# A SwiGLU block on one core: a split load of x, other PSUM banks for two small groups, and two sums of h moved

## The chip, the core and the metric

The kernel runs on one core of a Trainium2 chip. The core's engines work side by side and each has its own instruction queue, which it executes in order: TensorE (PE in the profile) for matrix products, VectorE (DVE), ScalarE (ACT) and GpSimd (POOL) for element-wise work, and SyncE (SP), whose queue issues most of the transfers. SBUF is the on-chip memory of 128 partitions, and PSUM the accumulators that TensorE writes, in eight banks of 128 x 512 fp32. Engines wait for each other by semaphores. The metric is the device time of one execution in microseconds.

## The reference

x has 2048 tokens of width 512, and the inner width is 1376. All inputs and the output are bf16.

```python
B, S, D, F = 1, 2048, 512, 1376
# x: (B, S, D)   w_gate, w_up: (D, F)   w_down: (F, D)
def reference(x, w_gate, w_up, w_down):
    g = silu(x @ w_gate)
    u = x @ w_up
    return (g * u) @ w_down
```

## The kernel before

x is brought in transposed (`xT_sb`), so that the contraction lies on partitions, in four chunks of 512 tokens: c = 0 to 3. F is cut into ten blocks of 128 (`ft` 0 to 9) and a tail of 96. Gate and up products of a block go into PSUM banks. ScalarE makes silu of the gate, and VectorE or GpSimd multiplies by up and writes h in bf16: `h0_sb` for tokens 0-1023, `h1_sb` for tokens 1024-2047.

Most products are made by Winograd's form of Strassen's scheme, with seven block products in place of eight for a 2 x 2 block problem. It needs sums of the weights (S1 to S4 and a cast A22) and sums of the tokens (T1 to T4 and a cast B22), kept as fp32r. In the gate/up phase a `Unit` (L581) treats two neighbouring blocks for two chunks of tokens. There are eight units: three for the first half of the tokens (u = 2, 4, 3) and five for the second (u = 0, 2, 4, 3, 1). The blocks 0 to 3 of the first half are made directly, by `classic` (L455). A unit's products run in the order p6, p5, p7, p2, then p1 of the next unit, then p3, p4. Banks X alternate between (0, 1) and (2, 3), Y is (4, 5), W is (6, 7). VectorE empties them: two `ts` sums for W after p5 and p7, an h product for Y, a copy of one X bank to Y, two more `ts` sums for W after p3, and an h product for X. GpSimd multiplies the `ts` sums into h.

The sums of weights are made by GpSimd into `ss_sb`, four slots that the units use in turn (`w_sums`, L531). The sums of tokens 0-1023 are made by VectorE into `tt_sb[0]`, those of tokens 1024-2047 by GpSimd into `tt_sb[1]` (`x_sums`, L555).

The down phase (`down`, L938) makes tokens 1024-2047 directly, tile by tile (`body`, L701), and tokens 0-1023 again by Strassen, in two `DownUnit`s (L833) whose operands are sums of w_down (S1 to S4, `s_sum`, L782) and sums of `h0_sb` (T1 to T4, `t_sum`, L796). Those sums lie in places that are free by then. S1 and S2 are made by GpSimd in the slot of u = 2, S3 and S4 by VectorE in the slot of u = 4. T1 and T2 are made by VectorE in `tt_sb[1]`, which the last unit still reads; T3 and T4 in `th_sb`, which shares its place with the weights `w_sb`. B22 lies in the slot of u = 3. Each T sum is three instructions: one block pair (128 x 512) and twice two (128 x 1024). `p1`'s result is read by VectorE (`keep`, the `r_sb` rows) before `p6` may add into the same bank.

The order of work on TensorE and SyncE is written out by hand (L992-L1038). For the other engines a planner (`Plan.schedule`, L58) works out an order from costs in ns, dependences and priorities: it always takes the operation that can start first. The T sums have the lowest priority, 9, so they go where an engine is idle in the plan. `land` is when the planner takes a load to have arrived; it changes the order only, the waits themselves are on semaphores.

Loads (L264-L319) are issued on SyncE in the order: xn (tokens 0-255), gate and up weights of the first blocks with tokens 256-511 between them, weights of blocks 2 and 3, tokens 512-1023 in one transposing load (`x1`, L293), and the rest. After the work on chunk 0, TensorE makes blocks 0, 1 and 2 of chunk 1 (L998), then the groups of the F tail, each in a bank b (L1013-L1020): `plan_x(c, b)` for its 96 gate columns and last 32 up columns of one chunk, and `plan_y(pi, b)` for its first 64 up columns of two chunks. Then come the units.

## Time and profile before

| | us |
|---|---|
| median of 3 runs | 116.96 (116.81 to 117.84) |
| the profiled execution, its own time | 116.91 |
| its span in the trace | 115.6 |
| TensorE busy | 111.7 |
| VectorE busy | 78.7 |
| ScalarE busy | 63.8 |
| GpSimd busy | 58.5 |

The profile is that of one execution. Each engine's busy time is the time in which it executes instructions other than waits. In the rows of the timeline the first number is the start from the beginning of the span, the second the length, both in us; then engine, line, operation, the tile written and those read, partitions x elements, and how many neighbouring instructions of one kind are merged in the row (x20). The bracket at the end gives the idle time before the row and what ended it. "PEld" is the loading of weights into TensorE, which overlaps its products. A row of the stretches has begin and end, length, then for PE, PEld, DVE, ACT and POOL the busy time and the number of instructions, then TensorE's granted clock (1.00 throughout here), the DMA share and GB/s.

### The profile page before, as it was taken

The numbers are of one execution on the slowest core, as the hardware profiler recorded it, in microseconds if no ns is written. First come the engines' busy times: TensorE is split into PE (matmuls) and PEld (weight loads), VectorE is DVE, ScalarE is ACT, GpSimd is POOL, SyncE is SP. The second block draws the span as 40 slices with busy tenths as digits, with TensorE's granted clock in tenths as the row PEclk, the third lists the DMA queues.
The fourth block names the chain that finished last, engine by engine and source line by source line (L and its number), as shares of the span: only waits on it lengthen the run. The fifth ranks groups of instructions, "written<-read, shape, count | busy, mean of one in ns | idle before, by whom it ended". The sixth has DMA issues, their size and how long they took to land.

```text
span 115.6 us, 1763 instructions
## 1 busy us (share of the span) xinstructions
PE 111.7 (97%) x650; PEld 69.0 (60%) x650; DVE 78.7 (68%) x115; ACT 63.8 (55%) x123; POOL 58.5 (51%) x55
## 2 busy tenths in 40 slices
PE   7999999999999999999999999999999799999993
PEld 2565566546675858576776858643435356866452
DVE  0122999773956859393949577599999997476423
ACT  5344765896778776767677787820767940000000
POOL 1069004999999999958999979144000000000000
PEclk9999999999999999999999999999999999999999
DMA  3999999993000000000000000000121002228896
GB/s 84 267 239 233 324 196 223 305 339 82 0 0 0 3 0 3 0 0 6 0 0 3 0 0 0 0 0 0 62 80 45 0 0 45 45 51 136 177 267 191
DMA packets 22776, 9.84 MB, mean 85 GB/s; under 512 B 12816, under 2 KB 22640, under 8 KB 22768
## 3 DMA queue, kind: packets, MB, share of 16 engines
q1 hardware_dynamic: 20624, 8.69, 31.2%
q10 hardware_dynamic: 2144, 1.05, 3.9%
q8 instruction: 5, 0.08, 0.3%
q14 instruction: 3, 0.02, 0.1%
HBM read 4.75 MB, written 2.10 MB: 59 GB/s over the span
## 4 chain that ended last, share of the span: by engine, by line
PE 72%; DVE 15%; DMA 7%; SPq 3%; issue 1%
PE psum L595 31%; PE psum L607 12%; PE psum L843 9%; DMA xT_sb<-in_x_dram 7%; PE psum L705 6%; DVE tt_sb L336 6%; PE psum L410 5%; DVE th_sb L336 4%; PE psum L474 3%; PE psum L855 3%; SPq L267 2%; PE psum L421 1%; PE psum L500 1%; DVE ss_sb L336 1%; SPq L279 1%
## 5 line engine op out<-in xcount | busy, mean ns | idle before, releaser
L595 PE MATMUL psum<-tt_sb,ss_sb 128*128 128x512 f32 x160 | 40.3, 404 | 0.0
L595 PEld LDWEIGHTS psum<-tt_sb,ss_sb 128*128 128x128 f32 x160 | 29.9, 188 | 7.8 <-DVE psum L325 0.4
L336 DVE TENSOR_TENSOR ts_sb<-r_sb,psum 128x512 f32<-128x512 f32 x32 | 20.5, 681 | 15.0 <-ACT r_sb L324 15.0
L336 POOL TENSOR_TENSOR h_sb<-sg_sb,ts_sb 128x512 bf16<-128x512 f32 x16 | 20.6, 1286 | 6.7 <-ACT sg_sb L331 6.7
L324 ACT ACTIVATE r_sb<-psum 128x512 f32<-128x512 f32 x32 | 17.3, 594 | 5.5 <-PE psum L595 5.5
L331 ACT ACTIVATE sg_sb<-psum 128x512 f32<-128x512 f32 x24 | 14.3, 598 | 10.7 <-PE psum L595 7.1
L336 DVE TENSOR_TENSOR h_sb<-sg_sb,psum 128x512 bf16<-128x512 f32 x24 | 16.4, 682 | 5.5 <-PE psum L410 5.5
L705 PE MATMUL psum<-wd_sb,h_sb 128*128 128x512 bf16 (+2 forms) x100 | 18.4, 337 | 0.0
L336 POOL TENSOR_TENSOR ss_sb<-w_sb 128x512 fp32r<-128x512 bf16 x10 | 11.4, 1157 | 13.5 <-DVE tt_sb L336 7.3
L607 PE MATMUL psum<-xT_sb,w_sb 128*128 128x512 bf16 x64 | 15.4, 381 | 0.0
L705 PEld LDWEIGHTS psum<-wd_sb,h_sb 128*128 128x128 bf16 x100 | 8.3, 98 | 9.2 <-issue 1.0
L410 PE MATMUL psum<-xT_sb,w_sb 128*64 128x512 bf16 (+1 forms) x128 | 12.8, 353 | 0.5 <-DMA xT_sb<-in_x_dram 0.3
L331 ACT ACTIVATE sg_sb<-ts_sb 128x512 f32<-128x512 f32 x16 | 10.1, 633 | 2.1 <-DVE ts_sb L336 2.1
L410 PEld LDWEIGHTS psum<-xT_sb,w_sb 128*64 128x64 bf16 x128 | 7.5, 110 | 5.4 <-issue 0.7
L607 PEld LDWEIGHTS psum<-xT_sb,w_sb 128*128 128x128 bf16 x64 | 5.5, 98 | 8.0 <-issue 2.5
L843 PE MATMUL psum<-tt_sb,ss_sb 128*128 128x512 f32 x20 | 5.6, 417 | 0.6 <-DVE r_sb L336 0.6
L325 DVE COPY psum<-psum 128x512 f32<-128x512 f32 x8 | 5.6, 699 | 0.7
L336 POOL TENSOR_TENSOR ss_sb<-w_sb,ss_sb 128x512 fp32r<-128x512 bf16 x5 | 5.8, 1169 | 0.2
L325 DVE CAST o_sb<-psum 128x512 bf16<-128x512 f32 (+2 forms) x6 | 3.0, 513 | 4.2 <-PE psum L705 3.1
L336 POOL TENSOR_TENSOR ss_sb<-ss_sb,w_sb 128x512 fp32r<-128x512 f32 x5 | 5.8, 1161 | 0.0
L843 PE MATMUL psum<-th_sb,ss_sb 128*128 128x512 f32 x20 | 5.5, 413 | 0.0
L855 PE MATMUL psum<-h_sb,wd_sb 128*128 128x512 bf16 x20 | 5.0, 381 | 0.0
(71 smaller groups left out, 121.7 us busy)
## 6 DMA issues: line engine op xcount, KB each, us to landing
wd_sb<-in_w_down_dram SPq DMA_DIRECT2D x1, 1280.0 KB, 9.0
w_sb<-in_w_gate_dram SPq DMA_DIRECT2D x4, 256.0 KB, 4.4
w_sb<-in_w_up_dram SPq DMA_DIRECT2D x4, 256.0 KB, 4.7
out_dram<-o_sb SPq DMA_DIRECT2D x7, 128.0 KB, 1.8
out_dram<-xT_sb ACTq DMA_DIRECT2D x4, 128.0 KB, 3.2
out_dram<-xT_sb ACTq DMA_DIRECT2D x2, 256.0 KB, 3.1
w_sb<-in_w_gate_dram SPq DMA_DIRECT2D x1, 352.0 KB, 5.2
w_sb<-in_w_up_dram SPq DMA_DIRECT2D x1, 320.0 KB, 5.7
```

Of the source, the lines that this page charges most:

```text
L267: lambda e: e.dma_start(w_sb[:, :, m, c0:c0 + f1 - f0], src[:, f0:f1].rearrange("(k p) f -> p k f", p=P)),
L324: return e.activation(out, src, ACT.Copy)
L325: return e.tensor_copy(out, src)
L331: "A", lambda e: e.activation(out, src, ACT.Silu), reads, writes, busy, A_LAG, prio
L336: engs, lambda e: e.tensor_tensor(out, a, b, alu), reads, writes, busy,
L410: ins = e.matmul(psum[h:h + HC, b, n0:n1], lhsT=w_sb[:, dk, m, ft * P + h:ft * P + h + HC], rhs=xT_sb[:, dk, c * SC + n0:c * SC + n1], sta ...
L474: ins = e.matmul(psum[m:m + HC, b, :], lhsT=w_sb[:, dk, 0, XC0 + m:XC0 + m + HC], rhs=xT_sb[:, dk, c * SC:(c + 1) * SC], start=(dk == 0), ...
L595: ins = e.matmul(bank(dst), lhsT=s[:, k, :], rhs=t[:, k, :], start=(start and k == 0), stop=(k == KH - 1), skip_group_check=True,)
L607: ins = e.matmul(bank(dst), lhsT=w_sb[:, k0 + k, m, f:f + P], rhs=xT_sb[:, k0 + k, c:c + SC], start=(start and k == 0), stop=(k == KH - 1) ...
L705: ins = e.matmul(psum[:, b, 0:c1 - c0], lhsT=hrows(F_ORDER[n], t, 0, P), rhs=wd_sb[:, F_ORDER[n], c0:c1], start=(start and n == n0), stop= ...
L843: ins = e.matmul(bank(dst), lhsT=self.ds[s][:, j, self.q, :], rhs=self.dt[t][:, j, :], start=(start and n == 0), stop=(n == NFF // 2 - 1), ...
L855: ins = e.matmul(bank(dst), lhsT=wd_sb[:, 2 * j + a, d * P:(d + 1) * P], rhs=h0_sb[:, 2 * j + a, 0:SC], start=(n == 0), stop=(n == NFF // ...
```

## The change

- Tokens 512-1023 are loaded by two transposing loads of 256 tokens, `x1a` and `x1b`. TensorE makes gate and up of blocks 0 and 1 for the first 256 of these tokens, four groups, and then for the other 256. Block 2 follows whole, as before.
- The tail groups use other banks: `plan_y(0)` 4 in place of 2, `plan_x(2)` 5 in place of 4, `plan_x(3)` 2 in place of 5.
- For the down blocks, T1 lies in the `ss_sb` slot of u = 4 and T3 in that of u = 3. Both are free before the last unit ends. Each is made of five instructions of 128 x 512. S3 and S4 move to the beginning of `tt_sb[1]`, B22 to `th_sb`. The order given is T1, T3, T2, S3, T4, S4.
- The planner's landing times are others, and eight semaphore numbers are no longer set aside, so that the loads take others.

```diff
-        s_out = [take(i) for i in (8, 1, 2, 3, 4, 5, 7, 6)]
...
-            plan.add(...).land = landed + (0 if landed < 5000 else 500 if landed < 10000 else 500)
+            plan.add(...).land = landed + 300
...
-                ... [name], 1500, 5.2 * (t1 - t0)
+                ... [name], 1500, (6.5 if SC <= t0 < 2 * SC else 4) * (t1 - t0)
...
-        load_x("x1", SC, 2 * SC)
+        for i in range(2):
+            load_x(f"x1{'ab'[i]}", SC + i * HT, SC + (i + 1) * HT)
...
         def x_keys(c):
+            if c == 1:
+                return ["x1a", "x1b"]
...
-            slots |= {n: (slot_of[U_ORDER[1][2]], i) for i, n in enumerate(("S3", "S4"))}
...
-            dt["T1"], dt["T2"], dt["T3"], dt["T4"] = tile(tt1, 0), tile(tt1, 1), th_sb[:, 0, :, :], th_sb[:, 1, :, :]
-            dt["B22"] = tile(flat(slot_of[U_ORDER[1][3]]), 0)
-            free = {"T1": before([("tt", 1, n, k) for n in X_SUM.values() for k in range(KH)])}
-            free["T2"] = free["T1"]
-            free["T3"] = free["T4"] = before([f"w{g}{a}" for g in "gu" for a, _ in slabs] + ["wut"])
-            free["B22"] = used(slot_of[U_ORDER[1][3]])
+            ds["S3"], ds["S4"] = wide(tt1, 0), wide(tt1, 1)
+            for n, u in (("T1", 2), ("T3", 3)):
+                dt[n] = tile(flat(slot_of[U_ORDER[1][u]]), 0)
+            dt["T2"], dt["T4"], dt["B22"] = tile(tt1, 1), th_sb[:, 0, :, :], th_sb[:, 1, :, :]
+            free = {n: used(slot_of[U_ORDER[1][u]]) for n, u in (("T1", 2), ("T3", 3))}
+            free |= {n: used(s) for n, (s, i) in slots.items()}
+            free["S3"] = free["S4"] = free["T2"] = before([("tt", 1, n, k) for n in X_SUM.values() for k in range(KH)])
+            free["T4"] = free["B22"] = before([f"w{g}{a}" for g in "gu" for a, _ in slabs] + ["wut"])
...
-                for j0, j1 in ((0, 1), (3, 5), (1, 3)):
+                for j0, j1 in ((0, 1), (3, 5), (1, 3)) if n in ("T2", "T4") else [(j, j + 1) for j in range(NJ)]:
...
             t_sum("T1")
+            t_sum("T3")
             t_sum("T2")
-            t_sum("T3")
-            s_sum("S3", "D", [t_ops["T3"]])
+            s_sum("S3", "D", [t_ops["T2"]])
...
-        for ft in early[:3]:
-            classic(1, [ft])
+        pairs = [(m, ft, next_bank()) for ft in early[:2] for m in range(2)]
+        for i in range(2):
+            for m, ft, b in pairs:
+                pe(
+                    gu_emit(m, ft, 1, b, range(KD), i * HT, (i + 1) * HT), [f"x1{'ab'[i]}", f"w{'gu'[m]}{slab_of[ft]}"],
+                    [("b", b)], 2,
+                )
+        for n, ft in enumerate(early[:2]):
+            classic_out(ft, 1, pairs[2 * n][2], pairs[2 * n + 1][2])
+        classic(1, early[2:3])
...
-        plan_y(0, 2)
-        y_out(0, 2)
-        plan_x(2, 4)
-        plan_x(3, 5)
+        plan_y(0, 4)
+        y_out(0, 4)
+        plan_x(2, 5)
+        plan_x(3, 2)
```

With this the planner gives VectorE the following order from the second last unit on (line numbers of the changed kernel; the `ss_sb<-h0_sb` rows are T1 and T3):

```
65 L336 TensorTensor ss_sb<-h0_sb 128x512 x4
66 L336 TensorTensor ts_sb0<-r_sb2,psum 128x512
67 L336 TensorTensor ts_sb1<-r_sb3,psum 128x512
68 L336 TensorTensor h1_sb<-sg_sb3,psum 128x512
69 L336 TensorTensor ts_sb2<-r_sb0,psum 128x512
70 L325 TensorCopy psum<-psum 128x512
71 L336 TensorTensor ts_sb3<-r_sb1,psum 128x512
72 L336 TensorTensor h1_sb<-sg_sb5,psum 128x512
73 L336 TensorTensor ss_sb<-h0_sb 128x512 x3
74 L336 TensorTensor ts_sb0<-r_sb0,psum 128x512
75 L336 TensorTensor ts_sb1<-r_sb1,psum 128x512
76 L336 TensorTensor h1_sb<-sg_sb1,psum 128x512
77 L336 TensorTensor ss_sb<-h0_sb 128x512
78 L336 TensorTensor ts_sb2<-r_sb4,psum 128x512
79 L336 TensorTensor ts_sb3<-r_sb5,psum 128x512
80 L336 TensorTensor h1_sb<-sg_sb2,psum 128x512
81 L336 TensorTensor ss_sb<-h0_sb 128x512 x2
82 L336 TensorTensor tt1_sb<-h0_sb,ss_sb 128x512
83 L336 TensorTensor tt1_sb<-h0_sb,ss_sb 128x1024 x2
```

GpSimd's order there is: an S1 sum, an h product, the other S1 sum, an h product, both S2 sums, then the last four h products. Before, an h product stood between the two S2 sums. In the first unit VectorE's bank copy (L325) comes ahead of an `hl`, the second `hty` and another `hl` product, where it stood behind the first two of these.

More of the change, by code (lines that the diff above doesn't have):

```diff
@@ L258, in load @@
             i = take(homes[name] if name in homes else rest[0])
-            plan.add("S", emit, writes=writes, busy=busy, lag=1800, dma=(i, 16)).land = landed + (0 if landed < 5000 else 500 if landed < 10000 else 500)
+            plan.add("S", emit, writes=writes, busy=busy, lag=1800, dma=(i, 16)).land = landed + 300
         slabs = [(0, 2), (2, 4), (4, 6), (6, 8), (8, NFF + 1)]
@@ L278, in load_x @@
             load(
-                name, lambda e: e.dma_start_transpose(xT_sb[:, :, t0:t1], xf[t0:t1, :]), [name], 1500, 5.2 * (t1 - t0)
+                name, lambda e: e.dma_start_transpose(xT_sb[:, :, t0:t1], xf[t0:t1, :]), [name], 1500, (6.5 if SC <= t0 < 2 * SC else 4) * (t1 - t0)
             )
@@ L770, in down_sums @@
             ds, dt = {}, {}
-            for n, (s, i) in slots.items():
-                ds[n] = flat(s)[:, i * HALF:(i + 1) * HALF].rearrange("p (j q c) -> p j q c", j=NJ, q=2)
+            wide = lambda a, i: a[:, i * HALF:(i + 1) * HALF].rearrange("p (j q c) -> p j q c", j=NJ, q=2)
             tt1 = tt_sb[1][:, :, :, :].rearrange("p n k c -> p (n k c)")
             tile = lambda a, i: a[:, i * NJ * SC:(i + 1) * NJ * SC].rearrange("p (j t) -> p j t", j=NJ)
-            dt["T1"], dt["T2"], dt["T3"], dt["T4"] = tile(tt1, 0), tile(tt1, 1), th_sb[:, 0, :, :], th_sb[:, 1, :, :]
-            dt["B22"] = tile(flat(slot_of[U_ORDER[1][3]]), 0)
-            free = {"T1": before([("tt", 1, n, k) for n in X_SUM.values() for k in range(KH)])}
-            free["T2"] = free["T1"]
-            free["T3"] = free["T4"] = before([f"w{g}{a}" for g in "gu" for a, _ in slabs] + ["wut"])
-            free["B22"] = used(slot_of[U_ORDER[1][3]])
+            for n, (s, i) in slots.items():
+                ds[n] = wide(flat(s), i)
+            ds["S3"], ds["S4"] = wide(tt1, 0), wide(tt1, 1)
[6 more added lines that the diff above has]
+            free["T4"] = free["B22"] = before([f"w{g}{a}" for g in "gu" for a, _ in slabs] + ["wut"])
             def s_sum(n, eng, after):
@@ L792, in s_sum @@
                         eng, at(n), a, b, alu, ["wd"] + [("ds", o, q) for o in of_], [("ds", n, q)], 9,
-                        1600 if eng == "G" else 780, used(slots[n][0]) + after,
+                        1600 if eng == "G" else 780, free[n] + after,
                     )
             def t_sum(n):
-                for j0, j1 in ((0, 1), (3, 5), (1, 3)):
+                for j0, j1 in ((0, 1), (3, 5), (1, 3)) if n in ("T2", "T4") else [(j, j + 1) for j in range(NJ)]:
                     at = lambda n: dt[n][:, j0:j1, :]
@@ L822, in casts @@
                 for q in range(2):
-                    cast_op("A", ds["A22"][:, :, q, :], wview[:, 1, 1, :, q, :], ["wd"], [("ds", "A22", q)], 9, 600, used(slots["A22"][0]) + after)
+                    cast_op("A", ds["A22"][:, :, q, :], wview[:, 1, 1, :, q, :], ["wd"], [("ds", "A22", q)], 9, 600, free["A22"] + after)
                 for j in range(NJ):
@@ L939, in down @@
             N2, N3 = NST // 2, NST // 2 + TPC
-            x_used = before([f"x{c}" for c in range(1, NSC)] + x_keys(0))
+            x_used = before([k for c in range(NSC) for k in x_keys(c)])
             for n0, n1 in ((0, NFF - 2), (NFF - 2, NFF)):
```

## The prediction

> **What bounds the kernel now.** I read the page's engine shares first, then the busy time by stretches, then the chain of waits. All times are of the profiled execution (span 115.6 us, its own time 116.91 us; the median of the runs, 116.96 us, is 0.05 us more, so sums against it carry over).

> ```profile
> PE 111.7 (97%) x650; PEld 69.0 (60%) x650; DVE 78.7 (68%) x115; ACT 63.8 (55%) x123; POOL 58.5 (51%) x55
> ```
> ```profile
> 25.40:74.60 49.20, 49.20 (x217) 34.34 (x216) 33.38 (x55) 36.64 (x72) 44.60 (x39) 1.00 0.04 8
> ...
> 76.00:91.40 15.40, 14.79 (x99) 6.30 (x97) 15.40 (x18) 8.56 (x16) 1.57 (x2) 1.00 0.11 35
> ```
> ```profile
> 4.75 7.56 DMA xT_sb<-in_x_dram
> 12.31 0.14 issue
> 12.45 5.37 PE psum L410 x48
> ...
> 90.70 0.61 DVE r_sb L336
> 91.31 0.04 issue
> 91.36 1.43 PE psum L843 x5
> ```

> TensorE (PE) is busy for 97% of the span. From 25.4 to 74.6 us it never stops (49.20 of 49.20 us), while GpSimd (POOL) is busy for 44.60 and VectorE (DVE) for 33.38. So a change gains only at the few places where PE stands, and it loses wherever it makes PE stand in the long middle. The chain shows two places: the load of x 512-1023 before 12.45, and VectorE before 91.36, at the end of a stretch where DVE works 15.40 of 15.40 us. How much each is worth comes from PE's timeline, because matmuls overlap and the idle shown is less than the time lost.

> ```profile
> 4.73 7.47 PE L410 MATMUL psum<-xT_sb,w_sb 128*64 128x256 bf16 x80
> 12.45 5.37 PE L410 MATMUL psum<-xT_sb,w_sb 128*64 128x512 bf16 x48 [0.25 <-DMA xT_sb<-in_x_dram]
> 17.62 1.92 PE L474 MATMUL psum<-xT_sb,w_sb 128*64 128x512 bf16 x16
> ...
> 25.34 3.51 PE L595 MATMUL psum<-tt_sb,ss_sb 128*128 128x512 f32 x12
> 28.69 1.90 PE L607 MATMUL psum<-xT_sb,w_sb 128*128 128x512 bf16 x8
> 30.24 5.01 PE L595 MATMUL psum<-tt_sb,ss_sb 128*128 128x512 f32 x20
> 35.09 1.90 PE L607 MATMUL psum<-xT_sb,w_sb 128*128 128x512 bf16 x8
> ...
> 68.30 4.91 PE L595 MATMUL psum<-tt_sb,ss_sb 128*128 128x512 f32 x20
> ...
> 73.74 2.21 PE L595 MATMUL psum<-tt_sb,ss_sb 128*128 128x512 f32 x8
> ...
> 89.93 0.82 PE L705 MATMUL psum<-wd_sb,h_sb 128*128 128x512 bf16 x3
> 91.36 1.43 PE L843 MATMUL psum<-tt_sb,ss_sb 128*128 128x512 f32 x5 [0.61 <-DVE r_sb L336]
> ```

> **x 512-1023 in two loads.** Without a wait a group starts 0.20 before the end shown for the one ahead (12.45 + 5.37 = 17.82, next at 17.62). The 80 matmuls end at 12.20, so the next could start at 12.00 and starts at 12.45: 0.45 us lost. Now the first half is enough to go on, and the second is needed 32 half matmuls later. The cost of halves: the 48 whole ones take 5.17 us from start to start, 0.108 each, so 32 whole ones cost 3.45 and 64 halves 3.45 at half price. From above: of the 80 in 7.27 us, 48 at 0.108 leave 2.10 for 32 halves, 0.066 each, which for 64 is 0.75 more; but that stretch holds waits of 0.3 and 0.2 us for loads (first two rows below), without which it is 0.05 each. I take 0, and 0 to 0.75 for the range.

> ```profile
> PEld psum L410 <- DMA w_sb<-in_w_up_dram: 0.3, 1, 0.3
> ...
> PEld psum L410 <- DMA xT_sb<-in_x_dram: 0.2, 1, 0.2
> ...
> PEld psum L595 <- DVE psum L325: 0.4, 1, 0.4
> ...
> PEld psum L595 <- DVE h_sb L336: 0.3, 1, 0.3
> ```
> ```profile
> 1.66 1.32 SPq L279 DMA_TRANSPOSE xT_sb<-in_x_dram  x1
> ...
> 4.75 3.91 SPq L279 DMA_TRANSPOSE xT_sb<-in_x_dram  x1
> ```

> On SyncE's queue the load holds 3.91 us as one piece; two pieces of 256 tokens hold between 2 x 1.32 and the same 3.91, so the loads queued behind it (weights, x 1024-2047) leave no later: 0. VectorE's sums of x need both halves and start when the whole would have landed: 0. Loads take other semaphores, the planner other landing times, and the two casts' tiles other homes: no instruction is added, 0. Gain 0.45.

> **Other banks.** The order of the changed kernel puts VectorE's bank copy (L325) ahead of two small products at the first unit. The 12 matmuls at 25.34 take 3.35 us to the next group, against 4.85 for 20 at 30.24, that is 2.91 for 12: 0.44 lost, by the last two waits quoted above. The first wait goes. The second, for the h product that frees bank 7, stays, as that product still stands behind the two small ones. I take 0.2 (0 to 0.44). The other tail groups get banks whose readers are one or more groups back: 0.

> **Two sums of h made early.** T1 and T3, ten VectorE instructions of 128x512, leave the stretch after 75 us. There they were these:

> ```profile
> 78.57 3.78 DVE L336 TENSOR_TENSOR tt_sb<-h_sb 128x512 fp32r<-128x512 bf16 x3
> ...
> 85.14 2.35 DVE L336 TENSOR_TENSOR th_sb<-h_sb 128x1024 fp32r<-128x1024 bf16 x2
> 87.41 0.68 DVE L336 TENSOR_TENSOR th_sb<-h_sb,tt_sb 128x512 fp32r<-128x512 bf16 x1
> ```

> Some 6.0 us leave (3.78 + 2.35, less overlaps). Two pieces of 0.6 stay, the first still blocked for about 0.8 as the first of the three is here (3.78 - 2.35 - 0.6). The second half of T4 (1.2) and the last two S4 sums (640 wide, by their width some 0.75 each) now come ahead of the r product that PE waits for. So that comes 6.0 - 2.0 - 2.7 = 1.3 us sooner, this wait goes, and what is late next is PE itself. It is worth 91.36 against 90.55 (89.93 + 0.82 - 0.20), 0.8, less the slower first step of such a group: I take 0.7 (0.6 to 0.8). Behind 91.36 the chain is PE to the end, so the gain lasts.

> The price is where the sums go. The order puts four T1 pieces behind the h product that here ends at 65.29, three more behind that of 70.91, and one where T3's first piece was already. VectorE runs in order: behind the four stand ts products that empty banks 6 and 7, and PE's group at 68.30 writes those.

> ```profile
> 64.61 0.68 DVE L336 TENSOR_TENSOR h_sb<-sg_sb,psum 128x512 bf16<-128x512 f32 x1
> 67.12 1.28 DVE L336 TENSOR_TENSOR ts_sb<-r_sb,psum 128x512 f32<-128x512 f32 x2 [1.83 <-ACT r_sb L324]
> ...
> 70.91 0.68 DVE L336 TENSOR_TENSOR h_sb<-sg_sb,psum 128x512 bf16<-128x512 f32 x1
> 73.42 1.29 DVE L336 TENSOR_TENSOR ts_sb<-r_sb,psum 128x512 f32<-128x512 f32 x2 [1.83 <-ACT r_sb L324]
> ...
> 75.22 1.63 DVE L336 TENSOR_TENSOR th_sb<-h_sb 128x512 fp32r<-128x512 bf16 x1
> ```
> ```profile
> 63.99 1.41 POOL L336 TENSOR_TENSOR ss_sb<-wd_sb 128x640 fp32r<-128x640 bf16 x1
> 65.37 1.28 POOL L336 TENSOR_TENSOR h_sb<-sg_sb,ts_sb 128x512 bf16<-128x512 f32 x1
> 66.61 1.39 POOL L336 TENSOR_TENSOR ss_sb<-ss_sb,wd_sb 128x640 fp32r<-128x640 f32 x1
> ...
> 69.97 1.42 POOL L336 TENSOR_TENSOR ss_sb<-ss_sb,wd_sb 128x640 fp32r<-128x640 f32 x1
> ```
> ```profile
> 75.03 1.28 POOL L336 TENSOR_TENSOR h_sb<-sg_sb,ts_sb 128x512 bf16<-128x512 f32 x1 [2.39 <-ACT sg_sb L331]
> ```

> The idle time is 1.83 us, and pieces alone take 0.68 and follow each other every 0.60 (two ts in 1.28). But the one sum of h that ran beside POOL took 1.63: POOL's product ended at 76.31, the sum at 76.85, so it did its 0.68 from 76.17 on, 0.14 before POOL's end, and nothing before. An instruction of VectorE that reads two SBUF tensors waits out POOL's. The ts and h products read one operand from PSUM and run undisturbed beside POOL (0.68 each).

> [...]

> At 65.29 POOL is full: it works on the S sum of 63.99, with the h product behind it, then two S sums back to back in the new order. Taking turns, on this trace's clock: T1's first piece holds from 65.26 (65.40 - 0.14), POOL's h product from 65.86 to 67.00 (0.60 later, 1.28 - 0.14), the second piece from 67.00, the S sum 67.60 to 68.85, the third piece from 68.85, the S sum 69.45 to 70.73, the fourth to 71.33. The first ts then ends at 72.01, where PE wanted its bank at 68.30: **3.7 us lost**. This takes POOL's rows to move with PE's when the early gains move those; if POOL stays, up to 0.65 more is lost here. At the second place POOL has only h products left, so one can block: 3 x 0.60 and up to 1.15 in an idle time of 1.9, ts up to 1.0 late, against some 0.75 of slack (ts ends 74.10, the last unit's four matmuls from 73.74 take about 1.1 first): 0 to 0.3, I take 0.15.

> Sum: 116.91 - 0.45 - 0.2 + 3.7 + 0.15 - 0.7 = **119.4 us**. With one POOL instruction fewer let in (1.25) it is 118.2; with no early gain, or with POOL staying, 120.1.

> **Rivals.**

> *VectorE keeps its turn.* Once it has the port, the four pieces run on end and POOL waits. For it: consecutive VectorE instructions overlap by 0.08 us, so POOL may find no gap; against it: 75.22 shows that a waiting engine gets the port at once, 0.14 before the other's end. The pieces then run from 65.26 to 67.66, ts ends at 68.34 instead of 68.30: 0.1 lost. POOL's delay costs nothing: the S sums it has still to make are first used at 91.36. 116.91 - 0.45 - 0.2 + 0.1 - 0.7 = 115.7 us, on the faster side. It decides from the second piece on: whether that starts 0.60 after the first or some 1.7.

> *Two and two.* The port changes hands only once in the group: two pieces to 66.46, POOL's h product to 67.60, two pieces to 68.80, ts to 69.48, 1.2 lost: 116.8 us.

> *The split does nothing.* If the first half lands no earlier than the whole (7.56 us of landing, all in one busy queue), PE waits at 12.00 as before and both early gains go, with VectorE keeping its turn: 116.3 us. Against it: the load is at the end of a queue that serves in order, and half of it needs only to be 0.3 us sooner.

> **How the numbers follow.** Taking turns 0.50 (119.4, own range 118.2 to 120.1), VectorE keeps its turn 0.33 (115.7, 115.3 to 116.3), two and two 0.10, no split 0.07. I put turns first because the one contended row shows a wait for a whole instruction, ended at once when the other was through. A measurement here can tell about 1% (1.17 us): below 115.8 is faster. Of the 0.33 some 0.20 lie below it, the rest with the 0.17 of the last two within 1%: faster 0.20, same 0.30, slower 0.50. The range runs from 115.5 to 120.1 and leaves out the low end of the second case and the high end of the first.

> **What would show it.** Right: T1 pieces in the VectorE rows near 65 us of 1.6 us and more each, PE idle 3 to 4 us for ts at the group now at 68.30, and no idle time before the groups now at 12.45 and 91.36. Wrong: four pieces in 2.5 us with POOL's h product stretched or moved instead; or PE's idle time where the small-product wait was, at 25 us, grown; or the 0.6 us before 91.36 still there, with T4 or a cast as its new cause.

## The result and the profile after

| | us |
|---|---|
| the changed kernel, median of 6 runs | 122.39 (121.36 to 123.49) |
| the kernel before beside it, median of 6 runs | 117.40 (116.63 to 119.45) |
| ratio, 95% interval | 1.040 (1.031 to 1.049): slower |
| the profiled execution, its own time and span | 123.49, 122.1 |

The forecast was 119.4 (115.5 to 120.1): the side and the mechanism came true, the size did not. The page of the changed kernel, its busy times and two rows of its 40 slices (each digit a busy share in tenths, and the clock granted to TensorE in tenths of full speed):

```profile
PE 114.1 (93%) x674; PEld 73.1 (60%) x682; DVE 84.0 (69%) x119; ACT 64.8 (53%) x123; POOL 59.9 (49%) x55
...
PE   7799999999999999999999907999999999999993
...
PEclk9999999999999999999999995899999999999999
```

PE's share fell from 97% to 93%: there is one hole, about 70 to 73 us, and right behind it two slices in which the clock was not full (digits 5 and 8). Before, every digit of the clock row was 9. The timeline of PE shows the same hole by its rows (start, length, ..., idle time and what ended it):

```profile
5.12 14.22 PE L412 MATMUL psum<-xT_sb,w_sb 128*64 128x256 bf16 x160 [0.68 <-DMA w_sb<-in_w_gate_dram]
...
25.33 1.89 PE L423 MATMUL psum<-xT_sb,w_sb 128*128 128x512 bf16 x8
...
31.82 4.54 PE L597 MATMUL psum<-tt_sb,ss_sb 128*128 128x512 f32 x18
...
68.33 1.90 PE L609 MATMUL psum<-xT_sb,w_sb 128*128 128x512 bf16 x8
73.93 6.38 PE L597 MATMUL psum<-tt_sb,ss_sb 128*128 128x512 f32 x20 [3.70 <-DVE ts_sb L336]
...
80.83 2.29 PE L597 MATMUL psum<-tt_sb,ss_sb 128*128 128x512 f32 x8
82.96 4.73 PE L707 MATMUL psum<-wd_sb,h_sb 128*128 128x512 bf16 x20
...
97.83 1.51 PE L847 MATMUL psum<-tt_sb,ss_sb 128*128 128x512 f32 x5
```

In this execution the first weights came late (the wait of 0.68) and the first products ran at half pace for longer (10 in the microsecond from 5 us on, 21 in the kernel before): the group at 25.33 starts at 23.49 in keep_busy3, a run of the next section with the same loads. These 1.8 us at the start are met with the loads of the kernel before too (early_t and banks_only below), and are left out by counting from anchors behind them. The anchors are groups that both traces have; the rows of before stand in the prediction, but for two, from the same view of the kernel before:

```profile
23.81 1.89 PE L421 MATMUL psum<-xT_sb,w_sb 128*128 128x512 bf16 x8
...
75.79 1.47 PE L705 MATMUL psum<-wd_sb,h_sb 128*128 128x512 bf16 x6
```

| stretch, start to start | before | after | difference |
|---|---|---|---|
| 23.81 to 30.24 (after 25.33 to 31.82), where the banks changed | 6.43 | 6.49 | +0.06 |
| to 68.30 (73.93), the group behind the first place | 38.06 | 42.11 | +4.05 |
| to 73.74 (80.83), the last unit's group | 5.44 | 6.90 | +1.46 |
| to 91.36 (97.83), the group that waited for r | 17.62 | 17.00 | -0.62 |
| to the end of the span | 24.24 | 24.27 | +0.03 |

That is +4.98. The gain of the split load lies ahead of the first anchor and is taken from the experiments (0.41, worked out below by the steps of the sum), so an undisturbed execution comes to 116.91 - 0.41 + 4.98 = 121.5 us. Three of the six runs took 121.36, 121.61 and 121.88.

The second largest line, +1.46, was in no step of the forecast. PE works all through it, only slowly, as the busy times by stretches show (begin and end, length, PE busy and matmuls, granted clock, DMA share, GB/s):

```profile
70.45:73.87 3.42, 0.00 (x0) 1.00 0.00 0
73.87:77.28 3.41, 3.35 (x8) 0.50 0.00 0
77.28:80.69 3.41, 3.34 (x16) 1.00 0.00 0
```

Behind the 3.42 us without a matmul the granted clock is 0.50 for 3.41 us: 8 matmuls where the next stretch has 16. PE's busy time cannot tell the two apart (3.35 and 3.34); the clock column and the count can.

The wait itself is made by VectorE and GpSimd. Their timelines in the changed kernel:

```profile
66.79 6.48 DVE L336 TENSOR_TENSOR ss_sb<-h_sb 128x512 fp32r<-128x512 bf16 x4
73.19 1.27 DVE L336 TENSOR_TENSOR ts_sb<-r_sb,psum 128x512 f32<-128x512 f32 x2
```
```profile
66.02 1.42 POOL L336 TENSOR_TENSOR ss_sb<-wd_sb 128x640 fp32r<-128x640 bf16 x1
67.39 1.74 POOL L336 TENSOR_TENSOR h_sb<-sg_sb,ts_sb 128x512 bf16<-128x512 f32 x1
69.08 3.64 POOL L336 TENSOR_TENSOR ss_sb<-ss_sb,wd_sb 128x640 fp32r<-128x640 f32 x2
```

Four sums that take 0.60 each alone took 6.40 from the first start to the ts product behind them, 1.6 each. GpSimd's instructions became longer too: 1.74 in place of 1.28, 1.8 in place of 1.39. Each stood for one sum of VectorE, then VectorE's next sum stood for it: turns, one for one, the four sums at 1.19, 1.77, 1.88 and 1.88. Of what the prediction calls the port, the traces show these waits and no more.

### The profile page after: what moved, and what is told of

Same layout as the page of the kernel before. It is cut to its first block, busy times and chain, and to the rows that moved or that the text cites. A ratio compares the mean times of both kernels' runs of the same rounds, so it can differ in the third digit from the quotient of the medians.

```text
span 122.1 us, 1821 instructions
## 1 busy us (share of the span) xinstructions
PE 114.1 (93%) x674; PEld 73.1 (60%) x682; DVE 84.0 (69%) x119; ACT 64.8 (53%) x123; POOL 59.9 (49%) x55
## 3 DMA queue, kind: packets, MB, share of 16 engines
HBM read 4.75 MB, written 2.10 MB: 56 GB/s over the span
## 4 chain that ended last, share of the span: by engine, by line
PE 77%; DVE 12%; issue 4%; DMA 3%; POOL 1%; ACT 1%; SPq 0%; POOLq 0%
PE psum L597 24%; PE psum L412 12%; PE psum L707 11%; PE psum L847 9%; PE psum L609 9%; DVE ss_sb L336 6%; PE psum L859 4%; DMA w_sb<-in_w_gate_dram 3%; PE psum L476 3%; DVE ts_sb L336 3%; PE psum L735 2%; DVE h_sb L336 2%; PE psum L423 1%; PE psum L502 1%; POOL h_sb L336 1%
## 5 line engine op out<-in xcount | busy, mean ns | idle before, releaser
L597 PE MATMUL psum<-tt_sb,ss_sb 128*128 128x512 f32 x160 | 41.8, 415 | 3.8 <-DVE ts_sb L336 3.7
L597 PEld LDWEIGHTS psum<-tt_sb,ss_sb 128*128 128x128 f32 x160 | 31.0, 196 | 12.4 <-DVE ts_sb L336 4.4
L336 DVE TENSOR_TENSOR ts_sb<-r_sb,psum 128x512 f32<-128x512 f32 x32 | 20.5, 680 | 11.2 <-ACT r_sb L324 11.1
L336 POOL TENSOR_TENSOR h_sb<-sg_sb,ts_sb 128x512 bf16<-128x512 f32 x16 | 21.1, 1320 | 10.9 <-ACT sg_sb L331 10.8
L336 DVE TENSOR_TENSOR h_sb<-sg_sb,psum 128x512 bf16<-128x512 f32 x24 | 16.4, 681 | 8.4 <-PE psum L412 7.6
L331 ACT ACTIVATE sg_sb<-psum 128x512 f32<-128x512 f32 x24 | 14.4, 599 | 14.2 <-PE psum L597 8.4
L324 ACT ACTIVATE r_sb<-psum 128x512 f32<-128x512 f32 x32 | 17.3, 595 | 5.5 <-PE psum L597 5.5
L336 POOL TENSOR_TENSOR ss_sb<-w_sb 128x512 fp32r<-128x512 bf16 x10 | 11.4, 1160 | 15.3 <-DVE tt_sb L336 8.9
L412 PE MATMUL psum<-xT_sb,w_sb 128*64 128x256 bf16 (+1 forms) x160 | 14.2, 348 | 0.7 <-DMA w_sb<-in_w_gate_dram 0.7
L609 PE MATMUL psum<-xT_sb,w_sb 128*128 128x512 bf16 x59 | 14.2, 380 | 0.4 <-issue 0.2
L331 ACT ACTIVATE sg_sb<-ts_sb 128x512 f32<-128x512 f32 x16 | 10.1, 633 | 5.8 <-DVE ts_sb L336 5.8
L412 PEld LDWEIGHTS psum<-xT_sb,w_sb 128*64 128x64 bf16 x160 | 10.9, 124 | 3.8 <-DVE xT_sb L325 0.9
L336 DVE TENSOR_TENSOR ss_sb<-h_sb 128x512 fp32r<-128x512 bf16 x10 | 13.0, 1348 | 0.0
L325 DVE COPY psum<-psum 128x512 f32<-128x512 f32 x8 | 5.6, 699 | 0.6
L336 POOL TENSOR_TENSOR ss_sb<-w_sb,ss_sb 128x512 fp32r<-128x512 bf16 x5 | 5.9, 1174 | 0.2
L325 DVE CAST o_sb<-psum 128x512 bf16<-128x512 f32 (+2 forms) x6 | 3.0, 512 | 4.2 <-PE psum L707 3.1
L336 POOL TENSOR_TENSOR ss_sb<-ss_sb,w_sb 128x512 fp32r<-128x512 f32 x5 | 5.8, 1168 | 0.0
L324 ACT ACTIVATE psum<-psum 128x512 f32<-128x512 f32 x8 | 4.8, 602 | 0.3 <-PE psum L609 0.2
L336 DVE TENSOR_TENSOR xT_sb<-r_sb,psum 128x512 bf16<-128x512 f32 x6 | 4.0, 687 | 1.2 <-PE psum L859 0.7
(74 smaller groups left out, 121.9 us busy)
```

The source lines that it names most:

```text
L324: return e.activation(out, src, ACT.Copy)
L325: return e.tensor_copy(out, src)
L331: "A", lambda e: e.activation(out, src, ACT.Silu), reads, writes, busy, A_LAG, prio
L336: engs, lambda e: e.tensor_tensor(out, a, b, alu), reads, writes, busy,
L412: ins = e.matmul(psum[h:h + HC, b, n0:n1], lhsT=w_sb[:, dk, m, ft * P + h:ft * P + h + HC], rhs=xT_sb[:, dk, c * SC + n0:c * SC + n1], sta ...
L597: ins = e.matmul(bank(dst), lhsT=s[:, k, :], rhs=t[:, k, :], start=(start and k == 0), stop=(k == KH - 1), skip_group_check=True,)
```

## The experiments

What each part is worth by itself came first.

**Without the sums of h (split_banks).** The changed kernel with T1 to T4, S3, S4 and B22 where and when they were before:

```diff
...
-            for n, u in (("T1", 2), ("T3", 3)):
-                dt[n] = tile(flat(slot_of[U_ORDER[1][u]]), 0)
...
+            dt["T1"], dt["T2"], dt["T3"], dt["T4"] = tile(tt1, 0), tile(tt1, 1), th_sb[:, 0, :, :], th_sb[:, 1, :, :]
...
```

> The split load, the half groups, the bank changes and the renumbered semaphores, with T1 to T4 as in the kernel before. Turns theory (the whole loss comes from the early sums): no wait before the first group on tokens 512-767, and 116.9 - 0.45 - 0.2 = 116.3 us, ratio 0.99 to 1.00. Rival (the halves cost: in the changed kernel's profile the L412 groups took 14.04 us from first to next against 12.89): 118 us, ratio 1.01, with the half groups slower than 0.054 us a matmul.

116.56 us, ratio 0.998 (0.995 to 1.002). PE's timeline in it:

```profile
4.39 12.83 PE L412 MATMUL psum<-xT_sb,w_sb 128*64 128x256 bf16 x160
...
24.75 1.75 PE L597 MATMUL psum<-tt_sb,ss_sb 128*128 128x512 f32 x6
26.65 1.66 PE L597 MATMUL psum<-tt_sb,ss_sb 128*128 128x512 f32 x6 [0.16 <-DVE h_sb L336]
28.16 1.90 PE L609 MATMUL psum<-xT_sb,w_sb 128*128 128x512 bf16 x8
...
90.82 1.43 PE L845 MATMUL psum<-tt_sb,ss_sb 128*128 128x512 f32 x5 [0.61 <-DVE r_sb L336]
```

All 160 products run without a wait for x. The 12 products of the first unit take 3.41 from 24.75 to 28.16, against 3.35 before: the first of two waits is gone and the second is longer by as much. The wait of 0.61 for r stays, so it is the sums of h that remove it. The slow-down needs those sums too. Against the kernel before beside it, 116.85, the two early parts are worth some 0.3 us, which the interval does not tell from nothing.

**The sums of h alone (early_t).** The kernel before with only that part of the change (the diff above, the other way round).

> Only the sums of h moved; loads, groups and banks as in the kernel before. Turns theory with the clock's fall: 116.9 + 3.9 (wait for ts) + 1.6 (half clock for 3.4 us behind it) + 0.15 - 0.7 = 121.9 us, ratio 1.04. Rival (a good part of the loss is the split's): below 120.7 us.

122.46 us, 1.049 (1.042 to 1.056). PE's timeline, VectorE's four sums listed by tile (count; shortest, median and longest in ns; first and last start), and GpSimd's timeline:

```profile
73.63 6.42 PE L595 MATMUL psum<-tt_sb,ss_sb 128*128 128x512 f32 x20 [3.71 <-DVE ts_sb L336]
```
```profile
L336 DVE TENSOR_TENSOR ss_sb<-h_sb x4: 677/678/4698, 66.5 to 72.3; 128x512 fp32r<-128x512 bf16 x4
```
```profile
65.25 1.41 POOL L336 TENSOR_TENSOR ss_sb<-wd_sb 128x640 fp32r<-128x640 bf16 x1
66.63 1.28 POOL L336 TENSOR_TENSOR h_sb<-sg_sb,ts_sb 128x512 bf16<-128x512 f32 x1
67.88 2.75 POOL L336 TENSOR_TENSOR ss_sb<-ss_sb,wd_sb 128x640 fp32r<-128x640 f32 x2
```

The whole loss is in this part. And here there were no turns: the first sum was out for 4.70 us, while GpSimd ran three instructions on end at their usual length; then came the other three sums at 0.68. The wait is the same within 0.01 (3.71, and 3.70 above), since either way all that GpSimd has queued lies ahead of the last sum. That it is so exactly the same is chance: from the end of GpSimd's S1 sum to the first ts product the order here took 6.24 us (66.66 to 72.90), the turns of the changed kernel 5.75 (67.44 to 73.19), but here GpSimd stood 0.45 earlier against PE. So "turns" was right for the changed kernel, but most of the price is set by the queue; the order was worth half a microsecond.

**GpSimd's S2 sums held back (s2_late).** The changed kernel, with S2 made to wait for the seventh early sum, so that only an h product can stand in the way:

```diff
-            s_sum("S2", "G", pool_after)
...
             t_sum("T3")
+            s_sum("S2", "G", [*pool_after, pieces[6]])
```

> The changed kernel with GpSimd's two S2 sums held until the seventh early piece is done, so that beside T1's four pieces GpSimd has only the rest of an S1 sum and one h product. Turns theory: the first two pieces take 1.2 and 1.8 us, the last two 0.68 each; TensorE waits about 1.3 us instead of 3.9, the clock stays at 1.00, 117.5 us. Rival (the pieces are slow in themselves, by their operands' places): 6.5 us for four as in the changed kernel and 121.5 us.

118.23 us, 1.013 (1.007 to 1.019). VectorE's and PE's timelines:

```profile
64.73 4.07 DVE L336 TENSOR_TENSOR ss_sb<-h_sb 128x512 fp32r<-128x512 bf16 x4
```
```profile
69.45 5.03 PE L597 MATMUL psum<-tt_sb,ss_sb 128*128 128x512 f32 x20 [1.27 <-DVE ts_sb L336]
...
75.00 2.56 PE L597 MATMUL psum<-tt_sb,ss_sb 128*128 128x512 f32 x8
77.40 4.78 PE L707 MATMUL psum<-wd_sb,h_sb 128*128 128x512 bf16 x20
```

Two GpSimd instructions fewer made the four sums 2.41 us shorter and the idle time 2.43 shorter. That settles GpSimd's instructions as the cause of the long sums; the rival, that the sums are slow by the places of their operands, is out, since those did not change. The granted clock stayed at 1.00. It is 0.7 us above its forecast of 117.5: 0.3 of that is the early gain, which is 0.35 and not 0.65, and as much the second place, where the last unit's 8 products take 2.40 (75.00 to 77.40) and before 2.05 (73.74 to 75.79).

**TensorE kept at work in the wait (keep_busy, keep_busy3).** The changed kernel with 13 products of a matrix of zeros put into PE's queue behind the group at 68.33. They add zero to a bank. The lines are those of keep_busy3:

```diff
+N_KEEP = 13
...
+        def keep(e):
+            for i in range(N_KEEP):
+                ins = e.matmul(bank(keep_bank), lhsT=zero_sb[:, :], rhs=ones_m, start=False, stop=False, skip_group_check=True)
...
```

> The changed kernel with 13 matmuls of zeros (128x512, adding nothing) into a bank of the next unit, put on TensorE in the place of the wait for ts; VectorE's and GpSimd's work is unchanged. If the clock falls because TensorE stands still: clock 1.00 behind the wait, matmuls of 0.23 us there, and 1.6 us less than the changed kernel, 119.9 us. Rival (the clock falls for another reason, such as the power drawn): 3.4 us at half clock as before and 121.5 us.

122.26 us, 1.048 (1.044 to 1.051), a miss: the planner, which saw the new products, also put an early sum of h ahead of VectorE's bank copy, and PE stood for that copy, by its timeline:

```profile
75.19 1.92 PE L601 MATMUL psum<-tt_sb,ss_sb 128*128 128x512 f32 x6 [0.56 <-DVE psum L328]
```

In keep_busy3 the products are put in after the planner is done, and every engine's order is that of the changed kernel.

> The run with zero matmuls kept the clock at 1.00 but was no faster: the planner had put one early sum ahead of VectorE's bank copy, and other orders differed. Here every engine's order is the changed kernel's, and only the 13 zero matmuls (and one fill of the zeros) are added. If TensorE's standing still lowers the clock and the low clock costs time: clock 1.00, and 1.0 to 1.6 us less than the changed kernel, 120.0 to 120.6 us. Rival (behind the wait VectorE is the bound anyway, so the low clock costs nothing): 121.6 us, with new idle time before TensorE's groups as long as what the clock gave.

121.40 us (120.48 to 122.74), 1.036 (1.029 to 1.044). By the totals alone that is within the interval of the changed kernel. PE's timeline tells more:

```profile
68.69 3.00 PE L1060 MATMUL psum<-const-bfloat16-1.0,zero_sb 128*128 128x512 bf16 x13 [0.30 <-ACT psum L326]
72.06 4.99 PE L599 MATMUL psum<-tt_sb,ss_sb 128*128 128x512 f32 x20 [0.37 <-DVE ts_sb L338]
...
77.58 2.60 PE L599 MATMUL psum<-tt_sb,ss_sb 128*128 128x512 f32 x8
80.02 4.73 PE L709 MATMUL psum<-wd_sb,h_sb 128*128 128x512 bf16 x20
...
94.87 1.50 PE L849 MATMUL psum<-tt_sb,ss_sb 128*128 128x512 f32 x5
```

The granted clock was 1.0 throughout. From 72.06 to 77.58 are 5.52 us, against 6.90 in the changed kernel: 1.38 us was the price of the low clock. From there to the group that used r, 17.29 against 17.00: 0.29 is given back, because at full clock PE comes to the second place early enough to stand there. Its 8 products take 2.44 (77.58 to 80.02), as in s2_late, and in the changed kernel 2.13 (80.83 to 82.96). Net, the low clock cost 1.09 us.

**Three sums in the first place (three).** The list names, for each early sum, the h product behind which it may run (11 is that of the first place, 13 of the second, 14 and 15 those of the last unit):

```diff
-                        ... free[n],
+                        ... free[n] + ([h_ops[hold[len(pieces)]]] if len(pieces) < len(hold) else []),
...
+            hold = [11, 11, 11, 13, 13, 13, 14, 15, 15, 15]
```

> The changed kernel with three early pieces instead of four in the first place; the fourth comes later. Turns theory: each piece less takes one turn of GpSimd away, 1.8 us, so TensorE waits 2.0 us there instead of 3.9. Whether the clock falls after 2.0 us is open (it did after 3.7, did not after 1.27): 118.3 us with the clock at 1.00, 119.9 us if it falls. Rival (the wait does not go by the number of pieces): above 120.5 us.

120.19 us, 1.031 (1.027 to 1.036). PE's timeline, and the busy times by stretches with the clock:

```profile
70.58 6.44 PE L598 MATMUL psum<-tt_sb,ss_sb 128*128 128x512 f32 x20 [1.88 <-DVE ts_sb L336]
```
```profile
67.33:70.74 3.41, 1.53 (x8) 1.00 0.00 0
70.74:74.15 3.41, 3.41 (x9) 0.50 0.00 0
```

Here the clock was 0.50 behind an idle time of 1.88 us, though PE was at work for 1.53 of the 3.41 us ahead of the fall; behind 1.27 us in s2_late it was 1.00. So one sum fewer shortened the wait by 1.8 us and left the price of the clock whole: 120.2 was measured, near the 119.9 forecast with a fall, not the 118.3 without one.

**One sum in the first place (spread, spread2).** Lists as above, with 11, 13, 13, 14 and six times 15; spread2 has 11, 13, 14 and seven times 15.

> The changed kernel with only one early piece in the first place (which fits beside one turn of GpSimd) and two in the second; the other seven come behind the last unit's h product. Turns theory: no wait for ts in the units, clock 1.00, and the wait of 0.6 us for the r product in the down phase gone, as VectorE has 1.8 us less to do there: 116.6 - 0.7 = 115.9 us, ratio 0.990 to 0.995. Rival (early pieces hurt wherever they stand, or the r product stays late): 116.6 us or more.

> As the run before, with one early piece in each of the first two places and eight later, so 1.2 us less in the down phase against some 0.8 us that the r product comes late. Turns theory: 115.9 to 116.2 us, ratio 0.990 to 0.998. Rival (the second place's two pieces cost nothing, and the r product needs all three): slower than the run before by 0.2 us or more.

spread: 116.34 us, 0.994 (0.990 to 0.998). spread2: 116.18 us, 0.992 (0.989 to 0.995). Both are faster than the kernel before, but by less than 1%. VectorE's and PE's timelines in spread:

```profile
65.00 1.05 DVE L336 TENSOR_TENSOR ss_sb<-h_sb 128x512 fp32r<-128x512 bf16 x1
66.79 1.29 DVE L336 TENSOR_TENSOR ts_sb<-r_sb,psum 128x512 f32<-128x512 f32 x2 [0.74 <-ACT r_sb L324]
...
77.24 5.37 DVE L336 TENSOR_TENSOR ss_sb<-h_sb 128x512 fp32r<-128x512 bf16 x7
```
```profile
67.97 4.91 PE L598 MATMUL psum<-tt_sb,ss_sb 128*128 128x512 f32 x20
...
90.48 1.42 PE L851 MATMUL psum<-tt_sb,ss_sb 128*128 128x512 f32 x5
```

One sum fits into VectorE's idle time with 0.74 us to spare, even when it stands for a GpSimd instruction. The group behind it follows without a wait, and seven sums run on end where GpSimd has little left. The wait for r is shorter, not gone: the r product ends at 90.43 (89.75 + 0.68) and the group at 90.48 starts behind it, 0.88 after the start of the group ahead, where it was 1.43 before and is 0.47 in spread2. These 0.4 us are about what spread lacks to its forecast of 115.9. In spread2, where the planner put the r product ahead of one more sum, it ends at 90.29 and PE starts at 90.76 without that wait; its 116.18 is within what was forecast.

**The two early parts one by one (split_only, banks_only).** The kernel before with only the two loads, and with only the other banks.

> The kernel before with the two loads of x 512-1023 alone (banks and sums of h as before). As on record: the 0.25 us of waiting before the second group goes and the unit's first group starts 0.37 to 0.45 earlier (about 22.5 us); the two small waits of 0.4 and 0.3 us after it stay, so the 20 matmuls of the next tail group start 7.3 us behind it as before. Rival, that the gain measured for both early parts together comes from the banks: the first unit group starts at 22.9 and the group after it closer by 0.4.

> The kernel before with the other banks of the tail groups alone. As on record: one of the two small waits behind the first unit's start goes, the other (on the h product) stays, so the group of 20 starts 0.2 us closer to the unit's start (7.1 in place of 7.3 us), and the wait for x at 12.3 us stays. If both go: 6.9.

119.24 and 119.06 us beside 117.85 for the kernel before, one execution each. Both had the late start described above, so they say nothing of the gain at the load. PE's timelines, of split_only and then of banks_only:

```profile
27.36 1.75 PE L597 MATMUL psum<-tt_sb,ss_sb 128*128 128x512 f32 x6
...
31.03 1.90 PE L609 MATMUL psum<-xT_sb,w_sb 128*128 128x512 bf16 x8
```
```profile
27.39 1.74 PE L595 MATMUL psum<-tt_sb,ss_sb 128*128 128x512 f32 x6
...
30.86 1.90 PE L607 MATMUL psum<-xT_sb,w_sb 128*128 128x512 bf16 x8
```

The first unit's 12 products take 3.67 with the split alone, 3.47 with the banks alone, 3.41 with both and 3.35 with neither. By these single executions the banks take back 0.26 of what the split loses there, and nothing without it. What both together come to, +0.06, is the firmer number: keep_busy3, spread and the changed kernel show the same stretch within 0.02 of it. In s2_late, where PE reached it some 0.24 later, it took 6.27: what PE gains ahead of it is in part lost to VectorE's h product there.

**When a sum is issued (late_piece, spread_late).** Why early_t had no turns: its first sum was issued at 66.5, some 0.2 us before GpSimd's S1 sum ended (65.25 + 1.41 = 66.66), that of the changed kernel 0.65 before (66.79 against 66.02 + 1.42). A memset on VectorE ahead of the first sum moves it:

```diff
+        late = Op("D", lambda e: e.memset(late_sb[:, :], 0.0), 0, 0, 0, None)
...
+        plan.order["D"].insert(plan.order["D"].index(plan.late_at), late)
```

> The changed kernel with a small memset on VectorE (about 0.5 us) ahead of the first early sum, so that this sum is issued some 0.1 us before GpSimd's S1 sum ends, as it was with the sums of h alone (0.18 before), and not 0.64 before. Theory: a sum that is issued that late loses the port to GpSimd's next instruction and gets none until GpSimd has nothing queued: first sum 4 to 4.7 us long, the other three 0.68 each, GpSimd's instructions at their usual 1.28 and 1.39. Rival: waiting engines take turns whenever both have work, and the other order came from something else in that kernel: sums of about 1, 1.77, 1.88, 1.88 us, GpSimd's 1.74 and 1.84. For the time the two are alike, as both put all three GpSimd instructions ahead of the last sum: a wait of 3.7 to 4.3 us for the ts product, 121.5 to 122.5 us.

> The faster variant (one early sum in the first place, two in the second, seven after the last unit) with a memset of some 0.37 us ahead of the first sum, so that it is issued about 0.1 us before GpSimd's S1 sum ends. If a late sum waits until GpSimd has nothing queued, this one sum waits for five GpSimd instructions on end (h, S2, h, S2, h), up to some 6 us, and TensorE stands for the ts products behind it: 3 us or more, near 120 us. If the engines take turns, it waits for one: 1.5 us in an idle time of 1.8, and 116.2 to 116.6 us.

123.52 and 118.13 us, one execution each, with the late start in both. VectorE's timelines, of late_piece and of spread_late:

```profile
67.58 5.97 DVE L338 TENSOR_TENSOR ss_sb<-h_sb 128x512 fp32r<-128x512 bf16 x4
```
```profile
67.32 0.84 DVE L338 TENSOR_TENSOR ss_sb<-h_sb 128x512 fp32r<-128x512 bf16 x1
```

The theory fell. In late_piece GpSimd's S1 sum ran from 66.28 for 1.43 us, so the first sum was issued 0.13 us before its end, and still the two took turns: 5.97 us for four, and an idle time of 3.69 on PE. In spread_late the one sum took 0.84. Why GpSimd ran three instructions on end in early_t stays open. None of the other runs shows it, and in it the wait was no longer (3.71).

## Why the prediction was right in kind and short in size

By the steps of the sum, with the table of anchors:

- **x in two loads**, -0.45 forecast, -0.41 measured. The wait goes, as said (160 products in one row). To size it, the start must be left out, as it differs between executions. Behind the first 32 products PE waits for a load of weights, and its weight loads behind that wait are an anchor; the rows are of the kernel before and of keep_busy3:

```profile
6.82 4.89 PEld L410 LDWEIGHTS psum<-xT_sb,w_sb 128*64 128x64 bf16 x48 [0.33 <-DMA w_sb<-in_w_up_dram]
```
```profile
6.91 10.11 PEld L414 LDWEIGHTS psum<-xT_sb,w_sb 128*64 128x64 bf16 x128 [0.23 <-DMA w_sb<-in_w_up_dram]
```
```profile
23.49 1.89 PE L425 MATMUL psum<-xT_sb,w_sb 128*128 128x512 bf16 x8
```

  From there to the group behind p1 are 16.99 before (6.82 to 23.81) and 16.58 in keep_busy3 (6.91 to 23.49). In split_banks, three and spread it is 16.58 as well, in spread2 16.57; in s2_late, which lost time to another load, 16.82. So the split is worth 0.41, and the half matmuls cost no more than the missing 0.04.
- **Other banks**, -0.2 forecast, +0.06 measured in that stretch. The step took the two waits for separate, and that is where it failed. The later one, for the h product, ends when VectorE gets there; without the first wait PE stands longer at it: in split_banks the second six products start 1.90 after the first six (24.75 to 26.65), where six take 1.45.
- **The first place**, +3.7 forecast, +4.05 measured. The mechanism is the forecast one, and *VectorE keeps its turn* (four sums in 2.4 us), *two and two* (1.2 us of wait) and *the split does nothing* are excluded by the rows above. That such a sum waits for GpSimd stood on the row at 75.22 (1.63 us, 0.68 alone), and what comes with more queued on no row of before; the runs show turns, with 1.19 to 1.88 us for each of the four, and in early_t one wait of 4.0 us. The 0.35 has the reason that the forecast named as a condition. Counted from the group at 30.24 (after 31.82), VectorE is free for the first sum at 34.97 in both (64.61 + 0.60 before, 66.79 after), but GpSimd's h product starts at 65.37 - 30.24 = 35.13 before and 67.39 - 31.82 = 35.57 after: GpSimd did not move with PE. That is 0.44 more, of which the turns, a little shorter than forecast, gave back 0.1.
- **The second place**, +0.15 forecast. In its own group it cost 0.08 here (2.13 less 2.05) and 0.4 at full clock (keep_busy3, s2_late), above the 0.3 that was its upper bound: PE reaches it late only because it ran slowly before. Another 0.25 is lost further on, which the forecast left out. VectorE leaves the second place late and comes to its next two ts products 1.32 after the start of the 20 products at 82.96, before 0.99 (76.78 less 75.79). So GpSimd's last h product is late too, and the last of the 20 wait for it. PE's weight loads there, before and after:

```profile
79.58 0.20 PEld L705 LDWEIGHTS psum<-wd_sb,h_sb 128*128 128x128 bf16 x2 [0.23 <-POOL h_sb L336]
```
```profile
87.09 0.11 PEld L707 LDWEIGHTS psum<-wd_sb,h_sb 128*128 128x128 bf16 x2 [0.56 <-POOL h_sb L336]
```

  In spread, with two sums there, this is not lost: 11.90 from its 20 products (75.46) to the group at 87.36, before 11.89 (75.79 to 87.68), in the changed kernel 12.14 (82.96 to 95.10).
- **The r product**, -0.7 forecast, -0.86 measured: its group starts 1.83 after the one ahead of it (96.00 to 97.83), before 2.77 (88.59 to 91.36), so 0.94 is gained, and the slower first step takes 0.08 of it. The -0.62 of the table is this 0.94 less the 0.08 and the 0.25 of the second place. That the two together come so near to the forecast is luck: each missed by some 0.17, one the other way.
- **The granted clock**: the step that failed most, a term put at nothing without a reason. The forecast let PE stand for 3.7 us and took it to go on at the pace of the rows before. It went on at half (0.50) for 3.41 us: +1.46, and 1.09 net of what is then hidden at the second place. This alone takes 119.4 to 120.5 and out of the range. All rows of before had the clock at 1.00, and from its first product on PE stood there for no longer than 0.61 us, so the profile of before could not price it. But the pace behind a wait of 3.7 us was then unknown, and the forecast needed bounds for it.

Together: the early parts gave 0.3 less, the first place cost 0.35 more, the clock 1.46 more, the second place 0.18 more, and the r product gave 0.16 more: 119.4 + 2.1 = 121.5.

## What to carry to other kernels

Ahead of a VectorE product that another engine waits for, count for extra sums with two SBUF operands not their own length alone, but also what GpSimd has queued there: here four sums of 0.60 each took 6.40 us beside the rest of an S1 sum and three more GpSimd instructions, and 3.99 beside that rest and one. Behind a long wait of TensorE, look for a low clock in the clock column and in the count of products, not in the busy share: here waits of 1.88 and 3.70 us were followed by 3.41 us at 0.50, worth 1.38 us in the changed kernel, and a wait of 1.27 us was not. A wait taken away just ahead of another one on the same releaser may be worth nothing until that one is moved too: here it gave +0.06 us for the -0.2 forecast.
